# A chunked mLSTM cell and an MLP: float64 weights converted on ScalarE and VectorE alone, beside the first up-blocks

## Chip, cores and metric

The kernel runs on one core of a Trainium2 chip. The metric is device time in microseconds, the median of several executions; a profiled execution gives the span from its first to its last instruction. The engines are PE (TensorE: matmuls, with PEld for its weight loads), DVE (VectorE), ACT (ScalarE), POOL (GpSimd) and SP (SyncE, which here only issues DMAs). Each works through its own queue in order and waits on semaphores.

## The reference, cut

```python
# q, k, v, o_gate: (4, 8, 768, 40) float32; i_gate, f_gate: (4, 8, 768)
for t in range(S):
    m_new = np.maximum(f_gate[:, :, t] + m, i_gate[:, :, t])
    f_stab = np.exp(f_gate[:, :, t] + m - m_new)
    i_stab = np.exp(i_gate[:, :, t] - m_new)
    m = m_new
    C = f_stab[:, :, None, None] * C + i_stab[:, :, None, None] * np.einsum('bhd,bhe->bhde', vt, kt)
    n = f_stab[:, :, None] * n + i_stab[:, :, None] * kt
    h_tilde = np.einsum('bhde,bhe->bhd', C, qt)
    nq = np.einsum('bhd,bhd->bh', n, qt)[:, :, None]
    denom = np.maximum(np.abs(nq), 1.0)
    o = 1.0 / (1.0 + np.exp(-o_gate[:, :, t]))
    y[:, :, t] = o * h_tilde / denom
# x = y as (4 * 768, 320); w_in (320, 2048) and w_out (2048, 320) are float64
h = x @ w_in
g = h * (1.0 / (1.0 + np.exp(-1.702 * h)))
return (g @ w_out).astype(np.float32)
```

## The kernel before

The sequence is cut into six windows of 128 steps. A window holds 128 steps of all four batches, so 512 tokens. Inside a window the recurrence is done as attention with a decay matrix, plus a product with the state carried over from the window before. The order of all work is written out by hand; each engine's queue gets its instructions in program order.

For each window and batch there are these steps. `transposes` turns k and q (tiles p_t in PSUM, copied to kT by ACT and to qT by DVE). `columns` turns the gate columns, and its last line takes an exponential of the output gate's tile eo, for the whole window at once. `weights` builds the decay matrix wt (p_w on PE, 32 exponentials a window on ACT). `scores` multiplies q and k (p_s) and DVE multiplies the result into wt. `values` forms p_o and then y, the gated output (den, eo and y on DVE). `seam` transposes y (p_x) into xT. `carry` updates the state (vw on POOL, p_c on PE, state on DVE). `gates` does the running sums and maxima of the next window on DVE.

The MLP of a window has eight blocks `up(w, j)`: 12 issued matmuls in the profile's count into two p_h tiles, two gelus on ACT into a tile g. Then come 16 steps `down(w, b, n)`, four blocks of f (128 rows of w_out) each, into p_out, a copy o_sb and a DMA. The attention of window w+1 is run beside `down` of window w. `carry` and `transposes` stand between the up-blocks. In window 0 nothing runs ahead of the attention, so that its whole chain (transposes to seam) stands before the first up-block.

The weights come as float64, as pairs of 32-bit words, cut into pieces. A piece is a DMA into a tile bits, and a conversion to float32 into w_in_sb, w_in_x or w_out_sb. Up-block j of window 0 needs pieces 0 to 2 (j = 0, 1), also 3 and 4 (j = 2, 3), also 5 to 7 (j = 4, 5) and also 8 and 9 (j = 6, 7). Pieces from 10 on are w_out. In the kernel before, ten w_out pieces make 20 in all.

A conversion takes two steps on ACT (`convert_a`, one piece ahead), five on DVE and two on POOL (`convert_b`), and then fetches the piece that is ten further. The tiles bits and g share one ring of ten buffers (tag "g"), and the PSUM tiles of the attention (p_t, p_w, p_s, p_o, p_x, p_c, p_cols) share four buffers (tag "a"), taken in turn: a matmul into one waits until the tile four places earlier has been read. By the addresses of the built program, g of up-block j of window 0 takes the buffer of piece 10 + j before the change.

Of the kernel before, what the change touches and what calls it, by code (L numbers as in the profile page):

```python
# [16 lines left out]
# The cell's recurrence in chunks of L steps. With F the running sum of f_gate from the chunk's start,  # L17
# a = i_gate - F and M = max(m at the chunk's start, running max of a), the cell's m is F + M, and
#   h[t] = sum over s <= t in the chunk of exp(a[s] - M[t]) (k[s].q[t]) v[s] + exp(m0 - M[t]) C q[t],
# n likewise as a further column of v that holds ones. All exponents are at most 0. Products are float32.  # L20
#
# A window is one chunk of all batches: B * L tokens. Its attention runs beside the MLP of the window before.
L = 128
NEG = -1.0e30

# The MLP's weights come as float64, which no engine takes: the kernel gets their bits and makes float32 of them,
# rounded to nearest. As float32 numbers the high words compare as the weights do; what is below float32's normal
# range becomes 0, and what is above its largest value.
HI_MIN = 1.125 * 2.0 ** -15  # 0x38100000, the high word of 2**-126
HI_MAX = 15 * 2.0 ** 13 - 2.0 ** -7  # 0x47EFFFFF, the last before that of 2**128  # L30
# [3 lines left out]
def kernel(  # L34
# [31 lines left out]
    op = ctx.enter_context(tc.tile_pool(name="op", bufs=3))  # L66
# [17 lines left out]
    def load(w):  # L84
        eo[w] = ld.tile([L, BH, D], FP, tag="eo", name="eo")
        for dst, src in ((k_st[w % 2], k), (q_st, q), (v_st[w % 2], v), (eo[w], o_gate)):
            nc.sync.dma_start(out=dst[:, :, 0:D],
                              in_=src[:, :, w * L:(w + 1) * L, :].rearrange("b h s d -> s (b h) d"))

    # Pieces of the weights: words, low and high in turn, and where their float32 goes.  # L90
# [12 lines left out]
    def piece_out(f, n, m0, m1):  # L103
        return w_out_sb[:, f:f + n, m0:m1], [(slice(0, 128), out_bits[:, f:f + n, 2 * m0:2 * m1])]
# [4 lines left out]
    for n in range(8):  # L109
        pieces += [piece_out(2 * n, 2, 0, 256)] + ([piece_out(2 * n, 8, 256, DM)] if n % 4 == 0 else [])  # L110
# [11 lines left out]
    load(0)  # L122
# [13 lines left out]
    # neg_mask[s, t] = NEG where s > t.  # L136
# [4 lines left out]
    # pick[32 j + r, bh] = -1 where r == bh: minus the sum of three rows of m3 to all partitions.  # L141
# [4 lines left out]
    # half[bh, p] = 1 where p is in the half of bh's parity, pair[bh, j] = 1 where bh // 2 == j.  # L146
# [10 lines left out]
    # The states' transposes, two heads a block: [keys, values and the ones] in the diagonal blocks.  # L157
# [8 lines left out]
    def words(n):  # L166
        lo, hi = bits[n][:, :, :, 0], bits[n][:, :, :, 1]
        return lo, hi, lo.bitcast(FP), hi.bitcast(FP), pieces[n][0]

    def convert_a(n):  # L170
        lo, hi, lo_f, hi_f, dst = words(n)
        A.activation(out=dst, in_=hi_f, func=AF.Square)
        A.activation(out=lo_f, in_=lo, func=AF.Copy, scale=2.0 ** -52)

    def convert_b(n):
        # The high word with 8 bits of exponent, then the low word by the power of two that its exponent stands for.
        lo, hi, lo_f, hi_f, dst = words(n)
        dst_u = dst.bitcast(U32)
        V.scalar_tensor_tensor(out=hi_f, in0=dst, scalar=HI_MIN * HI_MIN, in1=hi_f, op0=OP.is_ge, op1=OP.mult)
        V.tensor_scalar(out=hi_f, in0=hi_f, scalar1=HI_MAX, scalar2=-HI_MAX, op0=OP.min, op1=OP.max)  # L180
        V.tensor_scalar(out=dst_u, in0=hi, scalar1=3, scalar2=0x3FFFFFFF, op0=OP.logical_shift_left,
                        op1=OP.bitwise_and)
        V.scalar_tensor_tensor(out=hi, in0=hi, scalar=0xC0000000, in1=dst_u, op0=OP.bitwise_and, op1=OP.bitwise_or)
        V.tensor_scalar(out=dst_u, in0=hi, scalar1=0xFF800000, scalar2=None, op0=OP.bitwise_and)
        G.tensor_tensor(out=dst, in0=lo_f, in1=dst, op=OP.mult)
        G.tensor_tensor(out=dst, in0=hi_f, in1=dst, op=OP.add)

    def convert(n):
        if n + 1 < len(pieces):
            convert_a(n + 1)  # L190
        convert_b(n)
        if n + RING < len(pieces):
            fetch(n + RING)

# [1 line left out]
    def gates(w):  # L196
# [33 lines left out]
    def columns(w):  # L230
# [11 lines left out]
        A.activation(out=eo[w], in_=eo[w], func=AF.Exp, scale=-1.0)  # L242

# [32 lines left out]
    def values(w, b):  # L276
# [7 lines left out]
        if w:  # L284
# [7 lines left out]
            V.tensor_tensor(out=u, in0=po, in1=u, op=OP.add)  # L292
        den = work.tile([L, H, 1], FP, tag="den", name="den")
        V.tensor_scalar(out=den, in0=u[:, :, D:D1], scalar1=-1.0, scalar2=1.0, op0=OP.mult, op1=OP.max)
        V.tensor_tensor(out=den, in0=u[:, :, D:D1], in1=den, op=OP.max)
        z = eo[w][:, hs, :]
        V.scalar_tensor_tensor(out=z, in0=z, scalar=1.0, in1=den.to_broadcast([L, H, D]), op0=OP.add, op1=OP.mult)  # L297
        V.reciprocal(out=z, in_=z)  # L298
        y = ys[w, b] = work.tile([L, DM + 64], FP, tag="y", name="y")
        V.tensor_tensor(out=y[:, 0:DM].rearrange("p (h d) -> p h d", d=D), in0=u[:, :, 0:D], in1=z, op=OP.mult)  # L300
        G.tensor_copy(out=y[:, DM:DM + 64], in_=y[:, DM - 64:DM])  # L301

    def seam(w, b):
        if b == 0:
            xT[w] = work.tile([128, 3, B, L], FP, tag="xT", name="xT")
        px = ps_a.tile([128, 3, L], FP, tag="a", name="p_x")
        for c in range(3):
            T.transpose(px[:, c, :], ys[w, b][:, c * 128:(c + 1) * 128], ident)  # L308
        A.copy(out=xT[w][:, :, b, :], in_=px)  # L309
# [52 lines left out]
    # What needs the exponential, of the next window, stands beside the second product, that which needs the  # L362
    # gelu beside the first: the activation tables change twice a window.
# [13 lines left out]

    gates(0)
    convert_a(0)
    for b in range(B):  # L380
        transposes(0, b)
    load(1)
    n_in = RING
    for n, step in enumerate(attention(0)):
        run(step)
        if n:
            convert(n - 1)
    for n in range(n, n_in + 1):
        convert(n)
    for w in range(NW):  # L390
        more = w + 1 < NW
        for j in range(NF // 2):
            up(w, j)
            if w == 0:
                convert(n_in + 1 + j)
                if j == NF // 2 - 1:
                    convert(len(pieces) - 1)
            if more:
                if j == 0:
                    gates(w + 1)  # L400
# [4 lines left out]
        if w + 2 < NW:  # L405
            load(w + 2)
        side = attention(w + 1) if more else []
        for n in range(B * NF // 4):
            down(w, n // (NF // 4), n % (NF // 4))
            if n % 2 == 0 and side:  # L410
                run(side.pop(0))
# [32 lines left out]
```

## Time and profile before

| What | Value |
|---|---|
| median of 3 runs | 687.8 us (687.78 to 689.64) |
| span of the profiled execution | 686.1 us |
| PE busy | 617.4 us, 90% of the span |
| DVE / ACT / POOL busy | 266.6 / 173.5 / 91.3 us |
| DMA moved | 30.35 MB on SP's queue |

The span is the profiled execution's own time from the first to the last instruction; the median of the runs is 1.7 us above it. Busy lines give tenths of 40 equal slices of 17.2 us each; PEclk gives the granted clock of TensorE in the same way. A row of a timeline begins with its start in us from the span's start and its length; the bracket gives the idle time of that engine before it and what ended it. A row of stages gives for each engine the busy time and the number of instructions, then the granted clock, the DMA share and the rate.

### The profile page before, as it was taken

How to read it: one execution, taken by the hardware profiler on the slowest of the kernel's cores; microseconds unless marked ns; L12 is line 12 of the kernel's file. 1: busy time of each engine (PE TensorE's matmuls, PEld its weight loads, DVE VectorE, ACT ScalarE, POOL GpSimd, SP SyncE). 2: the span in 40 equal slices, each digit the busy share in tenths (PEclk: the TensorE clock that was granted, in tenths of full speed). 3: DMA queues.
4: the chain of work that ended last, by engine and by line, in shares of the span. 5: the costliest groups of instructions: out<-in, count | busy, mean ns of one | idle time of the engine just before them, and what ended most of it. 6: DMA issues, size and time to landing. Idle time of an engine off the chain costs nothing.

```text
span 686.1 us, 7417 instructions
## 1 busy us (share of the span) xinstructions
PE 617.4 (90%) x2950; PEld 390.1 (57%) x2950; DVE 266.6 (39%) x501; ACT 173.5 (25%) x404; POOL 91.3 (13%) x116
## 2 busy tenths in 40 slices
PE   2566317899999999999999999999999999999998
PEld 2454113357774457874457864467864467853475
DVE  3588994451663111663102562103561114630000
ACT  0642222253302242311233211242111242112200
POOL 2233653341002000011000011000011000000000
PEclk9755659999999999999999999999999999999999
DMA  9995220328000336000355000373000000000000
GB/s 138 312 164 165 92 62 0 39 27 99 11 10 11 39 41 85 11 11 10 39 58 67 11 21 0 40 76 49 11 20 0 1 3 14 5 20 0 0 20 19
DMA packets 108770, 30.81 MB, mean 45 GB/s; under 512 B 99456, under 2 KB 105600, under 8 KB 108736
## 3 DMA queue, kind: packets, MB, share of 16 engines
q1 hardware_dynamic: 108736, 30.35, 27.2%
q8 instruction: 23, 0.38, 0.2%
q14 instruction: 11, 0.09, 0.0%
HBM read 26.41 MB, written 3.93 MB: 44 GB/s over the span
## 4 chain that ended last, share of the span: by engine, by line
PE 78%; DVE 3%; issue 0%; POOL 0%; DVEq 0%
PE p_out L354 27%; PE p_h L341 22%; PE p_h L344 7%; PE p_o L282 5%; PE p_s L272 3%; PE p_t L250 3%; PE p_i L287 3%; PE p_c L319 3%; DVE eo L298 2%; PE p_w L258 1%; PE p_w L261 1%; PE p_x L308 1%; DVE u L291 0%; DVE u L292 0%; DVE y L300 0%; DVE eo L297 0%
## 5 line engine op out<-in xcount | busy, mean ns | idle before, releaser
L354 PE MATMUL p_out<-w_out_sb,g 128*128 128x320 f32 x768 | 216.6, 436 | 0.0
L341 PE MATMUL p_h<-xT,w_in_sb 128*128 128x512 f32 x384 | 179.9, 612 | 0.6 <-ACT xT L309 0.6
L354 PEld LDWEIGHTS p_out<-w_out_sb,g 128*128 128x128 f32 x768 | 142.6, 190 | 55.1 <-issue 0.8
L341 PEld LDWEIGHTS p_h<-xT,w_in_sb 128*128 128x128 f32 x384 | 71.8, 196 | 79.3 <-issue 71.2
L347 ACT ACTIVATE g<-p_h 128x512 f32<-128x512 f32 x96 | 52.1, 595 | 203.1 <-PE p_h L344 201.3
L265 ACT ACTIVATE wt<-p_w,cols 128x128 f32<-128x128 f32 x192 | 52.4, 386 | 94.2 <-PE p_w L261 94.2
L301 POOL COPY y<-y 128x64 f32<-128x64 f32 x24 | 6.0, 250 | 394.5 <-DVE y L300 394.5
L358 DVE COPY o_sb<-p_out 128x320 f32<-128x320 f32 x24 | 11.7, 486 | 120.0 <-PE p_out L354 120.0
L252 DVE COPY qT<-p_t 128x512 f32<-128x512 f32 x24 | 16.6, 691 | 98.9 <-PE p_t L250 98.9
L344 PE MATMUL p_h<-xT,w_in_x 64*128 64x512 f32 x192 | 54.2, 641 | 0.0
L319 PE MATMUL p_c<-vw,k_st 128*128 128x82 f32 x160 | 23.8, 295 | 31.7 <-POOL vw L315 31.7
L298 DVE RECIPROCAL eo<-eo 128x320 f32<-128x320 f32 x24 | 51.7, 2153 | 0.8
L282 PEld LDWEIGHTS p_o<-v_st,wt 128*128 128x128 f32 x384 | 50.7, 209 | 1.6 <-issue 0.2
L282 PE MATMUL p_o<-v_st,wt 128*128 128x41 f32 x384 | 51.3, 295 | 0.0
L319 PEld LDWEIGHTS p_c<-vw,k_st 128*128 128x128 f32 x160 | 20.6, 201 | 47.2 <-POOL vw L315 35.1
L309 ACT COPY xT<-p_x 128x384 f32<-128x384 f32 x24 | 11.5, 477 | 123.5 <-PE p_x L308 123.5
L291 DVE TENSOR_TENSOR u<-p_i,cols 128x328 f32<-128x328 f32 x20 | 10.0, 499 | 78.5 <-PE p_i L287 78.5
L274 DVE TENSOR_TENSOR wt<-p_s,wt 128x512 f32<-128x512 f32 x48 | 30.9, 682 | 14.3 <-PE p_s L272 14.1
L344 PEld LDWEIGHTS p_h<-xT,w_in_x 64*128 64x128 f32 x192 | 14.5, 184 | 36.4 <-issue 36.4
L330 DVE TENSOR_TENSOR state<-p_c,state 64x164 f32<-64x164 f32 x32 | 10.4, 326 | 63.5 <-PE p_c L319 63.3
L272 PE MATMUL p_s<-qT,kT 40*128 40x128 f32 x384 | 30.0, 299 | 0.0
L272 PEld LDWEIGHTS p_s<-qT,kT 40*128 40x128 f32 x384 | 25.2, 201 | 3.8 <-issue 2.4
(93 smaller groups left out, 480.7 us busy)
## 6 DMA issues: line engine op xcount, KB each, us to landing
bits<-in_moe_w_out_dram SPq DMA_DIRECT2D x10, 512.0 KB, 4.0
bits<-in_moe_w_in_dram SPq DMA_DIRECT2D x8, 512.0 KB, 7.7
k_st<-in_k_dram SPq DMA_DIRECT2D x6, 640.0 KB, 6.4
q_st<-in_q_dram SPq DMA_DIRECT2D x6, 640.0 KB, 6.7
v_st<-in_v_dram SPq DMA_DIRECT2D x6, 640.0 KB, 10.1
eo<-in_o_gate_dram SPq DMA_DIRECT2D x6, 640.0 KB, 10.2
out_dram<-o_sb SPq DMA_DIRECT2D x24, 160.0 KB, 1.8
bits<-in_moe_w_in_dram SPq DMA_DIRECT2D x4, 256.0 KB, 8.0
```

The source lines that it names most:

```text
L250: T.transpose(pt[:, p, :], src[:, h:h + 2, :].rearrange("p a b -> p (a b)"), ident)
L265: A.activation(out=x[:, i, p, :], in_=pw[:, p, :], func=AF.Exp, bias=cols[w][:, h:h + 1])
L272: T.matmul(pw[i][:, p, :], kT[w, b][r, p, :], qT[w, b][r, p, :], start=True, stop=True)
L274: V.tensor_tensor(out=wt[w, b][:, i], in0=pw[i], in1=wt[w, b][:, i], op=OP.mult)
L282: T.matmul(po[:, h, :], wt[w, b][:, i, p, :], v_st[w % 2][:, b * H + h, :], start=True, stop=True)
L287: T.matmul(pi[:, 2 * p:2 * p + 2, :].rearrange("p a b -> p (a b)"), qT[w, b][:, p, :], state[w % 2][:, b * NP + p].rearrange("p a b -> p ( ...
L298: V.reciprocal(out=z, in_=z)
L319: T.matmul(pc[:, p].rearrange("p a b -> p (a b)"), k_st[w % 2][:, h:h + 2, :].rearrange("p a b -> p (a b)"), vw[:, 2 * p:2 * p + 2, :].rea ...
L341: T.matmul(ph[i], w_in_sb[:, c, f * 128:(f + 1) * 128], x[:, c, :], start=(c == 0), stop=False)
L344: T.matmul(ph[i], w_in_x[r, j, :], x[r, 2, :], start=False, stop=True)
L347: A.activation(out=g[:, i, :], in_=ph[i], func=AF.Gelu_apprx_sigmoid)
L354: T.matmul(po, gs[w, f // 2][:, f % 2, b * L:(b + 1) * L], w_out_sb[:, f, :], start=(f == 0), stop=(f == NF - 1))
```

## The change

The conversion loses its POOL steps and becomes two steps on ACT and four on DVE, with an exact integer addition at the end. The w_out pieces become eight of 128 x 2 x 320, 18 pieces in all. Conversions are no longer interleaved with the first window's attention: pieces 0 to 2 stand beside its last seams, 3 to 15 beside up-blocks 0 to 6 (a table `beside_up` says which pieces are converted and which are fetched behind each block), and 16 and 17 beside the first two down steps. The first window's attention runs all weights and scores first and then all values and seams. `gates(1)` moves from block 0 to block 5. The load of the second window is cut in two parts: k and q after the first transposes, v and the output gate behind the fetches of block 1. The first window's 16 down steps go by halves of f: all batches with f 0 to 7, then all with f 8 to 15. The sigmoid is made of tanh (0.5 (1 + tanh(x/2))), and the reciprocal is taken of the eight denominators of a batch in place of 320 products. xT has one buffer for two, o_sb two for three.

```diff
-    def convert_a(n):
-        A.activation(out=dst, in_=hi_f, func=AF.Square)
-        A.activation(out=lo_f, in_=lo, func=AF.Copy, scale=2.0 ** -52)
-    def convert_b(n):
-        V.scalar_tensor_tensor(out=hi_f, in0=dst, scalar=HI_MIN * HI_MIN, in1=hi_f, op0=OP.is_ge, op1=OP.mult)
-        V.tensor_scalar(out=hi_f, in0=hi_f, scalar1=HI_MAX, scalar2=-HI_MAX, op0=OP.min, op1=OP.max)
-        V.tensor_scalar(out=dst_u, in0=hi, scalar1=3, scalar2=0x3FFFFFFF, op0=OP.logical_shift_left,
-        V.scalar_tensor_tensor(out=hi, in0=hi, scalar=0xC0000000, in1=dst_u, op0=OP.bitwise_and, op1=OP.bitwise_or)
-        V.tensor_scalar(out=dst_u, in0=hi, scalar1=0xFF800000, scalar2=None, op0=OP.bitwise_and)
-        G.tensor_tensor(out=dst, in0=lo_f, in1=dst, op=OP.mult)
-        G.tensor_tensor(out=dst, in0=hi_f, in1=dst, op=OP.add)
+    def convert(n):
+        A.activation(out=dst, in_=hi.bitcast(FP), func=AF.Abs)
+        A.activation(out=lo, in_=lo, func=AF.Copy, scale=2.0 ** -29)
+        V.tensor_scalar(out=dst, in0=dst, scalar1=HI_MIN, scalar2=HI_MAX, op0=OP.max, op1=OP.min)
+        V.tensor_scalar(out=dst_u, in0=dst_u, scalar1=3, scalar2=0x3FFFFFFF, op0=OP.logical_shift_left,
+        V.scalar_tensor_tensor(out=dst_u, in0=hi, scalar=0xC0000000, in1=dst_u, op0=OP.bitwise_and,
+        V.tensor_tensor(out=dst_u, in0=dst_u, in1=lo, op=OP.add)
...
-        A.activation(out=eo[w], in_=eo[w], func=AF.Exp, scale=-1.0)
+        A.activation(out=eo[w], in_=eo[w], func=AF.Tanh, scale=0.5)
...
+        V.reciprocal(out=den, in_=den)
         z = eo[w][:, hs, :]
-        V.scalar_tensor_tensor(out=z, in0=z, scalar=1.0, in1=den.to_broadcast([L, H, D]), op0=OP.add, op1=OP.mult)
-        V.reciprocal(out=z, in_=z)
+        V.scalar_tensor_tensor(out=z, in0=z, scalar=1.0, in1=u[:, :, 0:D], op0=OP.add, op1=OP.mult)
-        V.tensor_tensor(out=y[:, 0:DM].rearrange("p (h d) -> p h d", d=D), in0=u[:, :, 0:D], in1=z, op=OP.mult)
+        V.scalar_tensor_tensor(out=y[:, 0:DM].rearrange("p (h d) -> p h d", d=D), in0=z, scalar=0.5,
+                               in1=den.to_broadcast([L, H, D]), op0=OP.mult, op1=OP.mult)
...
-    load(1)
-    n_in = RING
-    for n, step in enumerate(attention(0)):
-        run(step)
-        if n:
-            convert(n - 1)
-    for n in range(n, n_in + 1):
-        convert(n)
+    load(1, 0)
+    columns(0)
+    for b in range(B + 1):
+        if b < B:
+            weights(0, b)
+        if b:
+            scores(0, b - 1)
+    for b in range(B + 1):
+        if b < B:
+            values(0, b)
+        if b:
+            seam(0, b - 1)
+            if b <= 3:
+                convert(b - 1)
+    beside_up = [((3, 4), (10, 11)), ((5, 6), (12, 13)), ((7, 8), (14,)), ((9, 10), (15,)), ((11, 12), (16,)),
+                 ((13, 14), (17,)), ((15,), ()), ((), ())]
...
+            blocks = [(b, n) for n0 in range(0, NF // 4, 2) for b in range(B) for n in (n0, n0 + 1)]
```

ACT at the program's start, before the change (kT, cols, eo, wt belong to the attention, the others to conversions):

```order
L172 ACT_TABLE_LOAD
L172 ACTIVATE w_in_sb<-bits 128x512
L173 ACTIVATE bits<-bits 128x512
L252 COPY kT<-p_t 128x512 x4
L239 ACTIVATE cols<-p_cols 128x64
L242 ACTIVATE eo<-eo 128x1280
L265 ACTIVATE wt<-p_w,cols 128x128 x8
```

and after it:

```order
L238 ACT_TABLE_LOAD
L238 COPY kT<-p_t 128x512 x4
L225 ACTIVATE cols<-p_cols 128x64
L228 ACTIVATE eo<-eo 128x1280
L251 ACTIVATE wt<-p_w,cols 128x128 x32
L297 COPY xT<-p_x 128x3x128
L172 ACTIVATE w_in_sb<-bits 128x512
```

The first conversion step has moved from ahead of the kT copies to behind all 32 exponentials and the first xT.

POOL around the first up-blocks, before (L185 and L186 are conversion steps, vw feeds p_c of `carry`):

```order
L185 TENSOR_TENSOR w_out_sb<-bits,w_out_sb 128x8x64
L186 TENSOR_TENSOR w_out_sb<-bits,w_out_sb 128x8x64
L315 TENSOR_TENSOR vw<-v_st_86,cols 128x328
L185 TENSOR_TENSOR w_out_sb<-bits,w_out_sb 128x2x256
L186 TENSOR_TENSOR w_out_sb<-bits,w_out_sb 128x2x256
```

and ACT behind the gelu of up-block 1 after the change, with buffer numbers (g_567 is up-block 2, bits_109 to bits_116 are pieces 5 to 8, g_601 is up-block 3):

```order
L335 ACTIVATE g_528<-p_h_521 128x512
L172 ACTIVATE w_in_sb_88<-bits_109 128x512
L173 ACTIVATE bits_109<-bits_109 128x512
L172 ACTIVATE w_in_sb_88<-bits_111 128x512
L173 ACTIVATE bits_111<-bits_111 128x512
L335 ACTIVATE g_567<-p_h_559 128x512
L335 ACTIVATE g_567<-p_h_560 128x512
L172 ACTIVATE w_in_x_89<-bits_113 128x512
L173 ACTIVATE bits_113<-bits_113 128x512
L172 ACTIVATE w_in_sb_88<-bits_116 128x512
L173 ACTIVATE bits_116<-bits_116 128x512
L335 ACTIVATE g_601<-p_h_593 128x512
```

vw has no conversion ahead of it on POOL any more, and two pieces' ACT steps stand between two gelus. By the addresses of the built program g of up-blocks 0 to 7 now takes the buffers of pieces 0, 3, 6, 8, 10, 12, 14 and 15.

DVE between the last block that has a state copy and the end of the up-blocks, after the change (the rows of w_out_sb are one piece, 15; ISA is the integer addition, over 1280 halves of 640 words):

```order
L208 TENSOR_TENSOR left_710<-left_705,part_707 32x128
L204 CAST part_712<-left_710 32x128
L205 COPY m3_701<-part_712 32x128
L213 TENSOR_TENSOR both_716<-m_end_163,m_run_692 32x1
L214 TENSOR_SCALAR dec_715<-pair_145,both_716 32x16
L238 COPY qT_731<-p_t_726 128x512
L174 TENSOR_SCALAR w_out_sb_90<-w_out_sb_90 128x640
L175 TENSOR_SCALAR w_out_sb_90<-w_out_sb_90 128x640
L177 SCALAR_TENSOR_TENSOR w_out_sb_90<-bits_616,w_out_sb_90 128x640
L179 ISA w_out_sb_90<-bits_616,w_out_sb_90 128x1280
L238 COPY qT_762<-p_t_757 128x512
L238 COPY qT_787<-p_t_782 128x512
```

and before it, the rows at the same place:

```order
L252 COPY qT_800<-p_t_795 128x512
L179 SCALAR_TENSOR_TENSOR bits_557<-w_out_sb_90,bits_557 128x512
L180 TENSOR_SCALAR bits_557<-bits_557 128x512
L181 TENSOR_SCALAR w_out_sb_90<-bits_557 128x2x256
L183 SCALAR_TENSOR_TENSOR bits_557<-bits_557,w_out_sb_90 128x512
L184 TENSOR_SCALAR w_out_sb_90<-bits_557 128x2x256
L252 COPY qT_834<-p_t_829 128x512
```

The qT copy of the second batch now stands behind the next window's gates, which stood ahead of the first state copy.

More of the change, by code (lines that the diff above doesn't have):

```diff
@@ L82, with load @@
     w_out_sb = const.tile([128, NF, DM], FP, name="w_out_sb")
-    def load(w):
-        eo[w] = ld.tile([L, BH, D], FP, tag="eo", name="eo")
-        for dst, src in ((k_st[w % 2], k), (q_st, q), (v_st[w % 2], v), (eo[w], o_gate)):
+    def load(w, part):
+        if part:
+            eo[w] = ld.tile([L, BH, D], FP, tag="eo", name="eo")
+        for dst, src in (((v_st[w % 2], v), (eo[w], o_gate)) if part else ((k_st[w % 2], k), (q_st, q))):
             nc.sync.dma_start(out=dst[:, :, 0:D],
@@ L121 @@
     nc.sync.dma_start(out=i_sb, in_=i_gate.rearrange("b h s -> (b h) s"))
-    load(0)
+    load(0, 0)
+    load(0, 1)
     for n in range(RING):
@@ L394 @@
             if w == 0:
-                convert(n_in + 1 + j)
-                if j == NF // 2 - 1:
-                    convert(len(pieces) - 1)
+                for n in beside_up[j][0]:
+                    convert(n)
+                for n in beside_up[j][1]:
+                    fetch(n)
+                if j == 1:
+                    load(1, 1)
             if more:
-                if j == 0:
+                if j == (5 if w == 0 else 0):
                     gates(w + 1)
```

39 lines of the change are left out of this document (17 added, 22 removed).

## The prediction

> **What bounds the kernel now.** I read the slices of the page first, then stages of the span, then who waits in the thin stage.
>
> ```profile
> PE   2566317899999999999999999999999999999998
> PEclk9755659999999999999999999999999999999999
> 67.00:74.00 7.00, 7.00 (x12) 2.57 (x12) 6.79 (x9) 5.63 (x10) 4.25 (x3) 0.68 0.22 76
> 74.00:99.50 25.50, 0.00 (x0) 0.00 (x0) 24.73 (x29) 3.47 (x5) 16.97 (x13) 0.59 0.29 83
> 99.50:150.50 51.00, 44.75 (x149) 21.76 (x150) 25.88 (x58) 15.41 (x29) 19.11 (x17) 0.91 0.12 13
> 500.00:600.00 100.00, 99.41 (x498) 63.01 (x498) 32.87 (x66) 25.06 (x60) 6.57 (x12) 1.00 0.02 7
> ```
>
> ```profile
> 94.43 1.08 ACT L347 ACTIVATE g<-p_h 128x512 f32<-128x512 f32 x2 [1.83 <-POOL w_out_sb L186]
> 98.62 0.85 POOL L315 TENSOR_TENSOR vw<-v_st,cols 128x328 f32<-128x328 f32 x1
> 99.53 2.00 PE L319 MATMUL p_c<-vw,k_st 128*128 128x82 f32 x8 [25.53 <-POOL vw L315]
> 150.45 2.32 PE L354 MATMUL p_out<-w_out_sb,g 128*128 128x320 f32 x8
> ```
>
> PE is full only from the ninth slice on; late in the run it is busy 99.4 of 100 us, so there no other engine's work can shorten anything. The loss is ahead of 150.45, where the first down product starts. Block 0 of up (67 to 74) is followed by 25.5 us without one matmul: DVE converts (24.73 busy), the gelu waits for a piece of w_out in its buffer, and vw, which p_c needs, stands behind the conversions on POOL. I forecast the new time of that down product and carry the rest over.
>
> **Durations that a conversion is made of.**
>
> ```profile
> 26.22 0.43 DVE L180 TENSOR_SCALAR bits<-bits 128x512 f32<-128x512 f32 x1
> 27.15 0.69 DVE L183 SCALAR_TENSOR_TENSOR bits<-bits,w_in_sb 128x512 uint32<-128x512 uint32 x1
> 68.06 1.63 POOL L185 TENSOR_TENSOR w_in_sb<-bits,w_in_sb 128x512 f32<-128x512 f32 x1 [2.15 <-DVE w_in_sb L184]
> 68.56 1.41 DVE L180 TENSOR_SCALAR bits<-bits 128x512 f32<-128x512 f32 x1
> ```
>
> A tensor-scalar step takes 0.43, but 1.41 where a POOL multiplication runs beside it. POOL's 40 conversion steps go, so I take 0.43. A new piece is on DVE two of these, one step with two operands (0.69), and the integer add, each with 0.03 between: the add is in no row. It reads two tensors of 512 words, as the 0.69 row does, but is issued over 1024 halves: 0.69 if two halves pass together, about 1.22 if singly (0.53 more at the 0.53 that 512 elements cost). I take 0.85, nearer to the row with the same bytes, and keep both ends. That makes 2.5 us a piece of w_in. A piece of w_out has 640 words; from 0.49 for 320 and 0.69 for 512 (rows below) 128 more cost 0.13, half that for tensor-scalar, 0.16 for the add: 2.95. Abs and Copy replace Square and Copy on ACT at the same 0.66 (row at 21.92), 0.56 apart.
>
> The Trainium skill (Vector Engine (DVE) Microarchitecture Reference, section 5.1) says that two-source instructions on 2-byte elements with unit steps pass two elements a cycle. By that rule the add would take 0.69, and the forecast would be about 2 us lower; no row here has such an instruction.
>
> **Start of block 0: 67.0 to 47.5.**
>
> ```profile
> 10.09 4.63 SPq L87 DMA_DIRECT2D eo<-in_o_gate_dram  x1
> eo<-in_o_gate_dram SPq DMA_DIRECT2D x1, 640.0 KB, 10.5
> 13.23 1.11 PE L250 MATMUL p_t<-ident,q_st 128*128 128x128 f32 x4 [3.57 <-DMA q_st<-in_q_dram]
> 21.92 0.66 ACT L172 ACTIVATE w_in_sb<-bits 128x512 f32<-128x512 f32 x1 [19.90 <-DMA bits<-in_moe_w_in_dram]
> 23.02 2.03 ACT L252 COPY kT<-p_t 128x512 f32<-128x512 f32 x4
> 25.74 1.26 ACT L242 ACTIVATE eo<-eo 128x1280 f32<-128x1280 f32 x1
> 26.90 2.17 ACT L265 ACTIVATE wt<-p_w,cols 128x128 f32<-128x128 f32 x8
> ```
>
> ACT's first Square waits for the first weights and holds the four kT copies to 23.0. It goes; q landed at 13.2, and eight transposes about 0.85 apart with their copies end near 19.6. What is late next is o_gate: it lands at 10.09 + 10.5 = 20.6, and the tanh (priced as the exponential, 1.26) stands ahead of the weights' exponentials on ACT. They start at 21.9, 2.0 per batch, nothing between them now: 29.9.
>
> ```profile
> 29.56 2.04 PE L282 MATMUL p_o<-v_st,wt 128*128 128x41 f32 x16
> 38.72 3.71 PE L282 MATMUL p_o<-v_st,wt 128*128 128x41 f32 x16
> 31.53 1.16 PE L272 MATMUL p_s<-qT,kT 40*128 40x128 f32 x16
> 42.35 2.08 PE L272 MATMUL p_s<-qT,kT 40*128 40x128 f32 x16
> 53.08 0.17 DVE L294 TENSOR_SCALAR den<-p_o 128x8 f32<-128x8 f32 x1 [2.82 <-PE p_o L282]
> 53.48 0.49 DVE L297 SCALAR_TENSOR_TENSOR eo<-eo,den 128x320 f32<-128x320 f32 x1
> 54.01 2.15 DVE L298 RECIPROCAL eo<-eo 128x320 f32<-128x320 f32 x1
> 56.26 0.49 DVE L300 TENSOR_TENSOR y<-p_o,eo 128x320 f32<-128x320 f32 x1
> 65.36 1.07 PE L308 MATMUL p_x<-ident,y 128*128 128x128 f32 x3 [4.14 <-DVE y L300]
> 66.47 0.48 ACT L309 COPY xT<-p_x 128x384 f32<-128x384 f32 x1 [7.08 <-PE p_x L308]
> ```
>
> The last scores need the last exponentials (their buffers): 1.16 warm, 2.08 cold, I take 1.6, to 31.5. Then p_o of batch 0, 2.04 to 3.71, I take 2.9, to 34.4. From there DVE sets the pace. A y costs two den steps (0.2 each with the gap), a reciprocal of 128x8 (between the 0.17 of a den step and 8/320 of 2.15 on top of it: 0.2), and two 0.49 steps: 1.65 where it was 3.7. DVE then runs y0, y1, piece 0, y2, piece 1, y3: 4 x 1.65 + 2 x 2.5 = 11.6, to 46.0. POOL's copy, p_x and xT (0.25 + 0.7 + 0.48) give 47.5. Piece 2 ends at 48.5; only the block's last two matmuls need it. All warm gives 46.2; all cold (each p_o 3.7, each p_x 1.07, DVE waiting for them, y3 at 50.7) 52.5.
>
> **Block 0 to the first down product: 76.4 to 47.9.** Block 0 itself I leave at 7.0, partly cold: end 54.5, from which t counts.
>
> ```profile
> 144.01 0.66 PE L250 MATMUL p_t<-ident,k_st 128*128 128x128 f32 x4
> 149.52 0.66 PE L250 MATMUL p_t<-ident,k_st 128*128 128x128 f32 x4
> 134.10 0.69 DVE L252 COPY qT<-p_t 128x512 f32<-128x512 f32 x1 [3.23 <-PE p_t L250]
> 2.94 0.41 DVE L202 TENSOR_TENSOR_SCAN f_run<-one,f_sb 32x128 f32<-32x128 f32 x1 [0.62 <-DMA f_sb<-in_f_gate_dram]
> 7.81 0.19 DVE L219 COPY m<-part 32x128 bf16<-32x128 bf16 x1
> ```
>
> PE needs 5.5 us per block with what stands behind it, 39.5 in all. DVE and the buffers need more. Gelu j may write only when the piece whose buffer it takes is converted (3, 6, 8, 10, 12, 14, 15 for j = 1 to 7), and the next two pieces' Abs stand behind that gelu on ACT: 1.8 from gelu's start to Abs done. A state or qT copy is 0.7; gates take 4.2 (the 5.1 seen from 2.94 to 8.0, less a wait and one slow step, plus the decay).
> - gelu 0, Abs: t = 1.8. Pieces 3, 4, state: 7.5. Pieces 5, 6: 12.5, state 13.2.
> - gelu 2 after piece 6, Abs 14.4; pieces 7, 8: 19.4. gelu 3, Abs 21.3; pieces 9, 10: 26.8, state.
> - gelu 4, Abs 28.8; pieces 11, 12: 34.7, qT. gelu 5, Abs 36.7; pieces 13, 14: 42.6; gates 46.8; qT 47.4.
> - The last p_t takes the buffer which that qT copy frees: 47.4, and 0.5 later the first down product.
>
> So DVE's queue, not PE, ends this stage, with PE idle near 8 us. The w_in pieces stay ahead of their blocks (piece 7 at 16.9, block 4 at 17.3). With the add at 1.22 the same steps end at 52.8, at 0.69 at 46. Fetches: pieces 12 and 13 wait on SP for pieces 4 and 5; then the loads of v and o_gate pass (4.63 each); piece 14 leaves near t = 20 and even 10.5 later is 6 ahead of its Abs. Hidden, as is w_out in eight fetches for ten.
>
> ```profile
> 101.32 5.81 PE L341 MATMUL p_h<-xT,w_in_sb 128*128 128x512 f32 x8
> 118.47 3.64 PE L341 MATMUL p_h<-xT,w_in_sb 128*128 128x512 f32 x8
> 153.11 4.57 PE L354 MATMUL p_out<-w_out_sb,g 128*128 128x320 f32 x16
> PE p_x L308 <- DVE y L300: 2.9, 5, 0.6
> ```
>
> **Behind it.** After a pause PE starts cold (5.81 for 3.64); a pause near 7 us ahead of down costs 2.2 again. Pieces 16 and 17 end at t = 62; in the new order the ninth group of four down steps needs them, eight groups of 2.3 after 47.9, with attention between: covered. The one xT buffer is written in down, after the last block has read it; the two o_sb are free again when the transfer of two groups earlier is out: nothing for either. The tanh brings no further table load in the program's order. In later windows the shorter y only removes the five waits of the last p_x: 2.9.
>
> **Sum.** Down product at 47.5 + 7.0 + 47.9 + 2.2 = 104.6 for 150.45: 45.9 less, and 2.9 less later. 686.1 - 48.8 = 637.3 of span. The median of the runs (687.8) stands 1.7 over the profiled span: 639.
>
> The Trainium skill (TensorE: Matmul & The Clock Gate, Part 1) has the clock drop after one idle window of about 3.4 us and return after one busy one. By that rule the waits near 2 us would stay warm and only the pause ahead of down is paid, as in the sum; attention paced by ACT could stay cold, the 52.5 of the start, and the time would be 644.
>
> **Rivals.**
> - The buffers bind less than I think and PE alone sets the blocks: 47.9 becomes 39.5 and the cold restart goes, 628. For it: POOL is empty. Against: DVE's own work there, 12 pieces (32), six state or qT copies (4) and gates (4), is 41 before any wait, so the add would have to be 0.69 as well.
> - The 1.41 comes from something other than POOL (the rows at 26.22 and 68.56 speak against it): 2 x 0.98 on 14 pieces, 27 more: 666.
> - Fetches late: if v and o_gate crawl, piece 14 arrives after t = 36.7; ten us late is 649, twenty 659.
> - Slower than before: the add runs like RECIPROCAL, 2153/320 = 6.7 ns an element, 6.9 us a piece. Fourteen pieces on the chain (9 of w_in, 5 wider) then cost over 90 more: about 730. It decides from an add of about 4 us. Against it: simple steps of two tensors all run near 1 ns.
> - Nothing gained: the conversions set the old pace. Only with two of these together.
>
> **Numbers.** Chances: forecast 0.78, PE alone 0.09, slow tensor-scalar 0.05, late fetches 0.04, slow add 0.03, nothing 0.01. Low end: warm start, add 0.69, no cold restart give 633.5; half of the PE rival brings 629. High end: cold start (+5), add 1.22 (+4.9), slow steps in gates (+2.3) give 651; a little of a late fetch, 654. That holds eight in ten. The runs before spread 0.3%, so 0.3% is about what can be told from nothing: faster 0.95, same 0.02, slower 0.03.
>
> **What would show it.** First wt exponential on ACT near 21.9, behind tanh; block 0 near 47.5; the add at 0.7 to 1.2 and tensor-scalars at 0.43; gelu 2 to 6 released by DVE, not by PE; first down product near 102 to 107; p_x without waits in later windows. The forecast falls if the add is above 1.5, if Abs waits for DMA, or if PE runs cold far beyond block 0.

## The result and the profile after

The changed kernel takes 639.48 us (median of 4 runs, 637.7 to 640.22) where the kernel before took 687.8 beside it (687.78 to 689.64): 0.9291 of the time, with a 95% interval of 0.9272 to 0.9309. The profiled execution has a span of 638.4 us for 686.1.

The page of the changed kernel, its line of busy times and the slices of PE and of the granted clock (16 us each):

```profile
PE 614.4 (96%) x2950; PEld 391.5 (61%) x2950; DVE 192.2 (30%) x473; ACT 173.7 (27%) x400; POOL 37.1 (6%) x76
...
PE   2898997999999999999999999999999999999997
...
PEclk9756997999999999999999999999999999999999
```

PE is busy 70% or more of every slice from the second on. The clock is another matter: slices two to four show 0.7, 0.5 and 0.6 though PE is busy there. The same by stages (span part, length, PE's busy time and instructions, granted clock, DMA share, GB/s):

```profile
20.00:25.00 5.00, 2.22 (x26) 1.00 1.07 311
25.00:30.00 5.00, 5.00 (x34) 0.50 1.02 389
...
35.00:40.00 5.00, 5.00 (x26) 0.50 1.38 175
55.00:60.00 5.00, 5.00 (x9) 0.58 0.38 131
60.00:65.00 5.00, 5.00 (x20) 1.00 0.00 0
```

PE pauses from about 20.8 to 23.0 and once more, for 0.55, up to 24.0. At 25.0 the clock falls, and from there PE runs without a gap until 50 and at half clock until 59; ahead of block 0 it waits 1.22 for the last y and 0.57 for xT. The timeline of that stretch and of the first up-block (start, length, engine, line):

```profile
21.82 4.23 ACT L251 ACTIVATE wt<-p_w,cols 128x128 f32<-128x128 f32 x16
30.87 3.79 PE L258 MATMUL p_s<-qT,kT 40*128 40x128 f32 x32
34.59 7.05 PE L268 MATMUL p_o<-v_st,wt 128*128 128x41 f32 x32
43.43 0.43 DVE L174 TENSOR_SCALAR w_in_sb<-w_in_sb 128x512 f32<-128x512 f32 x1 [0.28 <-ACT w_in_sb L172]
45.19 0.69 DVE L179 CUSTOM_DVE_ANT_0 w_in_sb<-bits,w_in_sb 128x1024 uint16<-128x1024 uint16 x1
52.94 6.77 PE L329 MATMUL p_h<-xT,w_in_sb 128*128 128x512 f32 x8 [0.57 <-ACT xT L297]
59.64 1.13 PE L332 MATMUL p_h<-xT,w_in_x 64*128 64x512 f32 x4
```

The p_o of two batches takes 7.05, at half clock throughout; a conversion's first step is back at 0.43 and the integer addition (CUSTOM_DVE_ANT_0) takes 0.69. Block 0 starts at 52.94 where it started at 67 before. The end of the up-blocks:

```profile
101.36 0.41 DVE L188 TENSOR_TENSOR_SCAN f_run<-one,f_sb 32x128 f32<-32x128 f32 x1
101.53 1.09 ACT L335 ACTIVATE g<-p_h 128x512 f32<-128x512 f32 x2 [3.19 <-DVE w_out_sb L179]
103.83 0.58 ACT L238 COPY kT<-p_t 128x512 f32<-128x512 f32 x1
104.46 1.11 PE L236 MATMUL p_t<-ident,q_st 128*128 128x128 f32 x4 [3.98 <-ACT kT L238]
105.37 4.47 PE L342 MATMUL p_out<-w_out_sb,g 128*128 128x320 f32 x8
105.57 0.67 DVE L238 COPY qT<-p_t 128x512 f32<-128x512 f32 x1
```

The gelu of block 6 waits for a w_out piece on DVE, the kT copy stands behind that gelu and the next Abs, and the last p_t waits 3.98 for it. Then down begins at 105.37 (150.45 before), at half clock. From there to the end, before and after in one row each (PE, PEld, DVE, ACT, POOL busy, clock, DMA share, GB/s):

```profile
150.45:686.10 535.65, 529.52 (x2579) 335.76 (x2577) 165.10 (x324) 126.08 (x304) 30.96 (x55) 1.00 0.19 26
```

```profile
105.37:638.40 533.03, 529.76 (x2578) 337.12 (x2577) 130.48 (x335) 128.41 (x307) 27.24 (x52) 1.00 0.19 27
```

So 45.1 us of the 47.7 came ahead of the first down product, and 2.6 behind it.

### The profile page after: what moved, and what is told of

Read it like the earlier page. It is cut to its first block, busy times and chain, and to the rows that moved or that the text cites. A ratio compares the mean times of both kernels' runs of the same rounds, so it can differ in the third digit from the quotient of the medians.

```text
span 638.4 us, 7322 instructions
## 1 busy us (share of the span) xinstructions
PE 614.4 (96%) x2950; PEld 391.5 (61%) x2950; DVE 192.2 (30%) x473; ACT 173.7 (27%) x400; POOL 37.1 (6%) x76
## 4 chain that ended last, share of the span: by engine, by line
PE 89%; DVE 4%; DMA 3%; ACT 2%; SPq 1%; issue 0%; DVEq 0%; ACTq 0%
PE p_out L342 33%; PE p_h L329 23%; PE p_h L332 7%; PE p_o L268 7%; PE p_s L258 5%; PE p_i L273 3%; PE p_c L307 3%; PE p_t L236 3%; PE p_w L244 2%; PE p_w L247 2%; DMA eo<-in_o_gate_dram 2%; PE p_x L296 1%; SPq L88 1%; DMA v_st<-in_v_dram 1%; ACT g L335 1%; DVE w_out_sb L177 1%
## 5 line engine op out<-in xcount | busy, mean ns | idle before, releaser
L329 PE MATMUL p_h<-xT,w_in_sb 128*128 128x512 f32 x384 | 177.4, 605 | 0.6 <-ACT xT L297 0.6
L236 PEld LDWEIGHTS p_t<-ident,k_st 128*128 128x128 f32 x96 | 11.7, 155 | 23.7 <-issue 23.7
L236 PE MATMUL p_t<-ident,k_st 128*128 128x128 f32 x96 | 17.2, 307 | 8.6 <-DMA k_st<-in_k_dram 8.6
```

The costliest lines, as they stand in the source:

```text
L236: T.transpose(pt[:, p, :], src[:, h:h + 2, :].rearrange("p a b -> p (a b)"), ident)
L329: T.matmul(ph[i], w_in_sb[:, c, f * 128:(f + 1) * 128], x[:, c, :], start=(c == 0), stop=False)
```

## The experiments

All of them are edits of the changed kernel. Spans are those of the profiled executions, to be compared with 638.4.

### What the parts are worth

**The old conversion in the new places.** The conversion's body is that of before (Square, Copy, five DVE steps, two POOL steps), the table `beside_up` and all else as changed.

```diff
-        A.activation(out=dst, in_=hi.bitcast(FP), func=AF.Abs)
+        A.activation(out=dst, in_=hi_f, func=AF.Square)
...
-        V.tensor_tensor(out=dst_u, in0=dst_u, in1=lo, op=OP.add)
+        G.tensor_tensor(out=dst, in0=lo_f, in1=dst, op=OP.mult)
+        G.tensor_tensor(out=dst, in0=hi_f, in1=dst, op=OP.add)
```

> Edit: the conversion as before the change (five DVE steps and two on POOL a piece), in the changed kernel's order and places. Theory A (the steps themselves set the pace: 4.65 us a piece on DVE before the change, two tensor-scalars of 1.40 among them beside POOL's products, for 2.45 now): twelve pieces 3 to 14 take 7 x 2.2 and 5 x 2.7 longer, 29 in all, less the 4 that DVE waited for ACT; first down product near 130, block 0 up to 3 later; span 660 to 668. Rival B (the order gave the gain: conversions spread beside the blocks hide behind PE whichever way they are made): span 638 to 648.

717.2 us, 1.0419 of before (1.0399 to 1.044): the new order with the old conversion is slower than the kernel before. Neither theory had that. Its timeline behind block 0:

```profile
66.30 0.66 ACT L173 ACTIVATE w_in_sb<-bits 128x512 f32<-128x512 f32 x1
69.93 1.62 POOL L181 TENSOR_TENSOR w_in_sb<-bits,w_in_sb 128x512 f32<-128x512 f32 x1 [8.91 <-issue]
70.44 1.40 DVE L176 TENSOR_SCALAR bits<-bits 128x512 f32<-128x512 f32 x1
75.95 1.29 POOL L182 TENSOR_TENSOR w_in_sb<-bits,w_in_sb 128x512 f32<-128x512 f32 x1
77.20 0.73 POOL L306 TENSOR_TENSOR vw<-v_st,cols 128x328 f32<-128x328 f32 x1
77.98 2.00 PE L310 MATMUL p_c<-vw,k_st 128*128 128x82 f32 x8 [14.01 <-POOL vw L306]
79.78 4.58 PE L332 MATMUL p_h<-xT,w_in_sb 128*128 128x512 f32 x8
100.03 4.69 PE L332 MATMUL p_h<-xT,w_in_sb 128*128 128x512 f32 x8
```

Block 1 stands behind p_c on PE, p_c waits for vw, and vw stands on POOL behind the conversion of two pieces, which begins behind the gelu of block 0. A block thus waits for a whole round through ACT, DVE and POOL: 20.3 us from one to the next (79.78, 100.03). In the changed kernel vw has nothing ahead of it on POOL. The row at 70.44 also shows the tensor-scalar at 1.40 again, beside a POOL product that runs from 69.93: the 1.40 does come from POOL.

**The old output gate.** Exponential on ACT, reciprocal of 128x320, as before.

```diff
-        A.activation(out=eo[w], in_=eo[w], func=AF.Tanh, scale=0.5)
+        A.activation(out=eo[w], in_=eo[w], func=AF.Exp, scale=-1.0)
...
-        V.reciprocal(out=den, in_=den)
...
+        V.reciprocal(out=z, in_=z)
```

> Edit: the output gate as before the change (exponential on ACT, reciprocal of 128x320 on DVE), all else as changed. Theory A (the gate's chain y, p_x, xT ends the steady windows and the first chunk): in the five later windows the wait of the last p_x comes back, 0.6 to 1.0 each, 3 to 5 in all; in the first chunk a y takes 3.7 for 1.5 on DVE, so DVE's 11 become 19.7 and block 0 begins 6 to 8 later; span 647 to 652. Rival B (PE's slow products set the first chunk and hide the longer y): only the later windows lose, span 641 to 643.

651.2 us (0.9458 of before, 0.9438 to 0.9479), span 649.2. Theory A. Block 0 begins 6.8 later, and from the first down product on the kernel takes 4.8 longer than the 533.03 above:

```profile
59.74 6.01 PE L328 MATMUL p_h<-xT,w_in_sb 128*128 128x512 f32 x8 [0.57 <-ACT xT L296]
```

```profile
111.38:649.20 537.82, 531.63 (x2578) 336.82 (x2577) 171.63 (x335) 128.25 (x307) 27.21 (x52) 1.00 0.19 27
```

```profile
PE p_x L295 <- DVE y L287: 2.9, 5, 0.6
```

The last row (who waits for whom: us in total, times, longest) is the wait that before had and the changed kernel has not. It is 2.9 of the 4.8; the other 1.9 is PE's busy time (531.63 for 529.76).

**The old order of the first window's attention.** One step of weights, scores, values and seams of successive batches, as before; pieces 0 to 2 in its last steps.

```diff
-    columns(0)
-    for b in range(B + 1):
...
+    for n, step in enumerate(attention(0)):
+        run(step)
+        if 4 <= n <= 6:
+            convert(n - 4)
```

> Edit: the first chunk's attention in the order of before (weights of batch s, scores of s-1, outputs of s-2, transposes of s-3 in one step), with pieces 0 to 2 converted in its last steps; all else as changed. Theory A (the order's lockstep costs waits, as before the change where PE stood still for some 10 of the 38 us between 29 and 67): block 0 begins at 56 to 60, span 642 to 646. Theory B (PE's cold products set the first chunk, and they are the same ones): block 0 within 1.5 of 52.9, span 637 to 640.

638.82 us (0.9278 of before, 0.9261 to 0.9295), span 637.9; block 0 at 53.38 for 52.94. Theory B: this part of the change is worth nothing that can be measured here. PE goes from 25 to 50 at half clock in both orders; what the order is worth at full clock was not tried.

**The natural order of the first down groups.**

```diff
-            blocks = [(b, n) for n0 in range(0, NF // 4, 2) for b in range(B) for n in (n0, n0 + 1)]
```

> Edit: the first window's down groups in their natural order (all four groups of a batch after one another), so that the fourth group needs pieces 16 and 17, which in the changed kernel are finished at 114.2 and 119.3. Theory A (the new order hides them): the fourth group would start near 115 and waits for piece 17, 4 to 5 us, span 642 to 644. Theory B (attention between the groups, at half clock, hides them anyway): no change, span 638 to 639.

644.25 us (0.9357 of before, 0.9341 to 0.9374), span 642.9, so the new order is worth 4.5. Theory A; the fourth group waits for piece 17:

```profile
119.53 5.19 PE L342 MATMUL p_out<-w_out_sb,g 128*128 128x320 f32 x12 [2.76 <-DVE w_out_sb L179]
```

The wait is 2.76 of the 4.5. The rest is PE at half clock behind it (0.50 from 120 to 123): these twelve products take 5.19, where 16 take 4.53 in the changed kernel.

### What sets the blocks

**Abs and Copy ahead of the block.** They leave their place behind gelu j.

```diff
+            if w == 0:
+                for n in beside_up[j][0]:
+                    convert_act(n)
             up(w, j)
             if w == 0:
                 for n in beside_up[j][0]:
-                    convert(n)
+                    convert(n, act=False)
```

> Edit: the Abs and Copy steps of the pieces that stand behind gelu j on ACT are put ahead of block j instead. Theory A (a loop sets the stage: a gelu waits on its buffer for a piece, the Abs of the next two pieces wait behind that gelu, and DVE waits about 1.1 us a block for them): the loop opens, DVE's waits for ACT go, pieces 3 and 4 are done during block 0, PE sets the blocks at some 5.5 us each. First down product 99 to 101 instead of 105.4, and its cold restart (2.3) goes too: span 631 to 634 for 638.4. Rival B (DVE's own work, about 40 us, sets the stage whatever the order): the first down product comes at most 2 us earlier, the pause ahead of it and the cold restart stay, span 636 to 638. Rival C (the early Abs find their weights not yet landed and hold the gelus back): slower, Abs waiting for DMA on ACT.

632.8 us (0.9189 of before, 0.9173 to 0.9206), span 631.1. Theory A, to the number. In the changed kernel DVE waited for these steps of ACT, and the gelus waited for DVE:

```profile
DVE w_in_sb L174 <- ACT w_in_sb L172: 9.1, 2, 8.0
DVE w_out_sb L174 <- ACT w_out_sb L172: 2.4, 2, 1.2
```

The 8.0 is one wait, for the Abs of piece 3 behind gelu 0; the others are near 1.1 a block. So the moved steps do two things: pieces 3 and 4 are converted while block 0 runs, and the wait in each later block goes. No run separates the two.

With the steps moved, such waits are gone, the gelus wait for PE alone, and down starts 5 us earlier and at full clock (2.32 for 4.47):

```profile
77.50 1.09 ACT L339 ACTIVATE g<-p_h 128x512 f32<-128x512 f32 x2 [1.99 <-PE p_h L336]
...
100.47 2.32 PE L346 MATMUL p_out<-w_out_sb,g 128*128 128x320 f32 x8
```

Block 0 ends at 60.8 in both; from there to down it is 39.7 us here and 44.6 in the changed kernel.

**No integer addition.** The low word is not added; its products and everything else stay.

```diff
-        V.tensor_tensor(out=dst_u, in0=dst_u, in1=lo, op=OP.add)
```

> Leaves out the integer addition of the low word in every piece (the weights lose their last bits), nothing else. If the chain of pieces sets the blocks, the twelve pieces 3 to 14 are each 0.69 (0.83 for w_out) and a gap of 0.1 shorter: about 10 us less chain, of which PE's own 39.5 us for the blocks lets 5 through, and the cold restart of 2.3 goes as well: first down product at 99 to 101, span 631 to 633. If DVE does not set the stage: no change, 638. Block 0's start: earlier by up to 1.6 if DVE sets it (two pieces stand ahead of the last y), unchanged at 52.9 if PE's slow products do.

631.89 us (0.9177 of before, 0.9159 to 0.9196), span 629.7; first down product at 99.06, at full clock, block 0 from 52.71 to 59.3.

```profile
99.06 2.32 PE L341 MATMUL p_out<-w_out_sb,g 128*128 128x320 f32 x8
```

So the chain of pieces did set the blocks: taking some 10 us out of it brings them to PE's own 39.8, and no further. Block 0's start does not move: there it is not DVE that sets the pace. Block 0 itself is 1.2 shorter, because in this execution the clock rose at 56.4 and not at 59.2.

**The gates one block later.**

```diff
-                if j == (5 if w == 0 else 0):
+                if j == (6 if w == 0 else 0):
```

> Edit: the gates of the second window stand behind block 6 instead of block 5 on DVE. The prediction's step (the last p_t takes the buffer which the qT copy behind the gates frees, so the 4.2 of gates lie on the path): the first down product comes up to 4 us earlier, at 101 to 102, span 634 or less. The reading of the trace after (the last p_t takes the buffer which the kT copy on ACT frees, behind gelu 6, which waits for piece 14; pieces 13 and 14 stand ahead of the gates): no change, first down product 105 to 106, span 638 to 639; if anything slower, since the columns of the second window need the gates.

642.68 us (0.9331 of before, 0.9307 to 0.9355), span 641.0: slower by 2.6, which neither reading gave. The last p_t and with it the first down product come earlier (102.21 for 105.37), near what the prediction's step gave, but the second down group stands behind the gate columns on PE, and these now wait for the gates:

```profile
101.72 0.65 PE L236 MATMUL p_t<-ident,q_st 128*128 128x128 f32 x4 [1.62 <-DVE qT L238]
102.21 2.32 PE L342 MATMUL p_out<-w_out_sb,g 128*128 128x320 f32 x8
107.84 0.27 PE L218 MATMUL p_cols<-ident,st 96*128 96x96 f32 x1 [3.32 <-DVE st L198]
110.06 0.60 PE L222 MATMUL p_cols<-dec,half 32*128 32x16 f32 x2 [1.95 <-DVE dec L214]
```

The edit also changes which buffer the last p_t takes. By the addresses of the two built programs it is here the buffer of q of batch 1, four places earlier, which the qT copy frees at 101.7; in the changed kernel it is that of k of batch 2, three places earlier, which the kT copy frees at 104.4. So the rule "taken in turn, four places earlier" of the section on the kernel does not hold for that tile, and the gates at block 5 are not free: they do not stand in the chain that ends at the first down product, but with them out of the way of that qT copy it begins 3.2 earlier. At block 6 they cost more than that: the waits of 3.32 and 1.95, and a group at half clock behind them.

### What sets the start

**The tanh behind the exponentials.**

```diff
-        A.activation(out=eo[w], in_=eo[w], func=AF.Tanh, scale=0.5)
+        if w:
+            A.activation(out=eo[w], in_=eo[w], func=AF.Tanh, scale=0.5)
...
+    A.activation(out=eo[0], in_=eo[0], func=AF.Tanh, scale=0.5)
     for b in range(B + 1):
         if b < B:
             values(0, b)
```

> Edit: the first window's tanh of the o_gate stands behind all 64 exponentials of the weights on ACT instead of ahead of them. Theory A (the exponentials on ACT, held by the tanh and the landing of o_gate, set the start): exponentials begin near 20.0 instead of 21.8, block 0 begins 1.8 earlier at 51.1, span 636.6. Theory B (from the first scores at 30.9 on, PE's own cold products set the start): the scores may begin up to 1.8 earlier too, so the same gain, unless DVE's y, which now waits for the tanh near 31, or kT and qT copies hold them: then block 0 stays at 52.9. The two agree if PE starts with the exponentials; they part if the scores stay at 30.9.

632.15 us (0.9192 of before, 0.915 to 0.9233), span 629.1. Block 0 begins at 46.34, 6.6 earlier and not 1.8. PE's pause is gone (0.31 for 2.23 ahead of the first scores), and the clock stays full until 32.3, 2.3 after p_o began:

```profile
25.00:30.00 5.00, 4.76 (x59) 1.00 1.03 383
30.00:35.00 5.00, 5.00 (x34) 0.73 1.08 249
35.00:40.00 5.00, 5.00 (x27) 0.50 1.39 206
```

The same scores that took 3.79 for two batches take 1.16 a batch here. That raised the question whether the 1.8 on ACT or the clock gave the gain.

**Ten idle matmuls in the pause.** Their result is read by nobody.

```diff
+    def warm(k):
+        pd = ps_m.tile([128, W], FP, tag="m", name="p_d")
+        for i in range(k):
+            T.matmul(pd, ident_b, neg_mask.unsqueeze(1).to_broadcast([L, NP, L]), start=(i == 0), stop=(i == k - 1))
...
             weights(0, b)
+        if b == 1:
+            warm(10)
```

> Edit: ten 128x512 bfloat16 matmuls into a spare PSUM tile are put on PE behind the weights' products of batch 1, where PE in the changed kernel stands still from 20.7 to 23.0. Their result is not read. Theory A (that pause makes the clock fall at 25.0): the clock stays at 1.00 through the scores, p_s and p_w run at full speed as in the run with the late tanh (clock full until 32.3, block 0 at 46.3), and block 0 begins 1.7 later than there because the exponentials begin 1.7 later: 48.0 for 52.9; span 633 to 634. Theory B (the clock falls because the scores with 40 rows and the weights' products load PE lightly, pause or not): the fall stays near 25, block 0 at 52.9 or a little later, span 638 to 639.

633.07 us (0.9205 of before, 0.9173 to 0.9238), span 631.8, block 0 at 47.03. The ten products, the clock while the scores run, and block 0:

```profile
20.63 2.32 PE L370 MATMUL p_d<-neg_mask,ident_b 128*128 128x512 bf16 x10
30.00:35.00 5.00, 4.80 (x53) 1.00 1.08 264
47.03 6.29 PE L329 MATMUL p_h<-xT,w_in_sb 128*128 128x512 f32 x8 [0.57 <-ACT xT L297]
```

Theory A: useless products that fill the pause, and nothing else changed, give 5.9 us at the start, and each of the four runs (632.51 to 636.95) is below each of the changed kernel's (637.7 to 640.22). So of the late tanh's 6.6 most is the clock.

**And six more ahead of each step of p_o and p_x.**

```diff
+        warm(6)
         if b < B:
             values(0, b)
         if b:
             seam(0, b - 1)
```

> Edit: the ten matmuls of the run before, and six more of them ahead of each of the five steps of p_o and p_x in the first chunk. Theory A (41 columns a product keep the clock down though PE is never idle, wide products keep it up): the clock stays at 1.00 to block 0; p_o takes 2.0 a batch for 3.5, six matmuls 1.3 a step, so PE needs 3.9 a step and DVE (four y of 1.5, two pieces of 2.45) 11 in all: last y near 44.8, block 0 near 46.5 and 4.8 long for 7.8, its end near 51 for 60.7; span 628 to 630. Theory B (the clock falls in this stretch whatever PE does): six matmuls cost 2.6 a step at half clock, block 0 later than 52.9, span above 640.

634.66 us (0.9207 of before, 0.9179 to 0.9236), span 633.5, where 628 to 630 was expected. In this execution the ten products ended 0.91 ahead of the first scores, the clock fell at 26.7 all the same, and the gain of the run before was lost: filling the pause does not keep the clock every time. But the question it was made for is answered:

```profile
34.09 2.74 PE L370 MATMUL p_d<-neg_mask,ident_b 128*128 128x512 bf16 x6
36.63 2.02 PE L268 MATMUL p_o<-v_st,wt 128*128 128x41 f32 x16
39.78 1.87 PE L268 MATMUL p_o<-v_st,wt 128*128 128x41 f32 x16
...
52.24 3.70 PE L329 MATMUL p_h<-xT,w_in_sb 128*128 128x512 f32 x8 [0.57 <-ACT xT L297]
```

With 512-column products between them the clock rises at 36.9, in the middle of the attention, and p_o runs at 1.87 a batch to the end for 3.48; block 0 takes 3.70 for 6.77 in its first eight.

### A faster version

**Late tanh and early Abs together**, and the same with six idle matmuls a step:

> Two edits together: the first window's tanh behind the exponentials of the weights, and Abs and Copy of the pieces ahead of their block on ACT. If the two gains are of different places (start of block 0: 9.3 of span; blocks and cold restart: 7.3, of which the late-tanh run may already hold part of the restart), block 0 begins near 46.3, the first down product 39 to 40 after block 0's end at 92 to 93, span 621 to 624. If the earlier start moves the blocks into the landing of the weights (Abs waiting for DMA), the gains overlap: span 625 to 629.

> As the run before, with six 128x512 bfloat16 matmuls, whose result is not read, ahead of each of the five steps of p_o and p_x. From the run with kept clock: p_o 1.87 for 3.48 and block 0 4.8 for 6.8 to 7.8 long. If the clock is still full at 30 (as with the late tanh), the first p_o ends near 33.4, DVE's 11 us set the rest, block 0 begins at 45 to 46 and ends near 50.5 for 52.6: span 2 us under the run before, 619 to 622. If the matmuls only take PE's time: the same or up to 3 longer.

The first takes 625.58 us (median of 6 runs, 624.66 to 629.71; 0.9103 of before, 0.9077 to 0.9129), span 623.1, block 0 at 46.30 and down at 92.45, at full clock:

```profile
92.45 2.32 PE L347 MATMUL p_out<-w_out_sb,g 128*128 128x320 f32 x8
```

The two gains lie in different places and add up, 13.9 us under the changed kernel. The second takes 626.75 (626.38 to 627.71; 0.9106, 0.9092 to 0.9121), span 625.3, and is not faster: the clock had fallen at 24.6, ahead of the first of its idle matmuls, with block 0 at 50.19. Up to there the two programs are the same.

## Why the prediction held, and where it was wrong

The time came out at 639.5 for 639.0, but that it came so close is luck: terms that were too small and terms that were too large cancelled. Step by step, in the prediction's own terms:

- **First exponential near 21.9, behind the tanh.** 21.82. Right: with the tanh behind them the exponentials begin at 20.17. But that is 1.65 earlier, and block 0 came 6.6 earlier, so most of it is the clock.
- **Start of block 0, 47.5: wrong by 5.4.** It was 52.94. The step that failed is the choice of a middle between warm and cold durations (at full and at half clock) for p_s and p_o ("I take 1.6", "I take 2.9"). There was no middle in the profiled execution: the clock fell at 25.0 and all that followed ran cold, as in the bound of 52.5 that I had worked out and given as the high end. The sentence on the clock rule of the Trainium skill (TensorE: Matmul & The Clock Gate, Part 1) had put 52.5 beside an attention that stays cold, and so it came; the total of 644 that went with it did not, because of the terms below. What that rule was taken to say of the waits, that near 2 us they would stay warm, did not come: the clock fell 2.0 us after the end of a wait of 2.23. With the middle fell "from there DVE sets the pace": without the addition, DVE has less to do and block 0 starts within 0.3 us of the same place (52.71).
- **Block 0, 7.0.** 7.8, for the same reason.
- **Block 0 to the first down product, 47.9.** 44.6. The mechanism, that a gelu waits for a piece and the next Abs for that gelu, is shown by the moved Abs (39.7, PE's own pace, where the prediction had 39.5 for PE) and by the run without addition. Two terms were off. The addition was priced at 0.85 and takes 0.69, for which the prediction itself had 46. And the last step named the wrong releaser: the last p_t took the buffer which the kT copy on ACT freed at 104.4, not the one of the qT copy behind the gates, which began only at 105.6. That the gates' place holds the first down product back was still near the truth: one block later, it comes 3.2 earlier.
- **Cold restart of down, 2.2.** 4.47 for 2.32: right, though the pause ahead of it was 3.98 and not near 7.
- **Behind it, 2.9 less.** 4.8 less by the run with the old gate; the p_x waits were counted, PE's busy time was not. With the cold restart that gives the 2.6 between the rows above.
- **Sum.** 5.4 and 0.8 too little, 3.3 and 1.9 too much: 638.4 for 637.3.

Of the rivals, "PE alone sets the blocks" did not hold for this change, but one move of two ACT steps made it hold. The slow tensor-scalar from another cause than POOL is refuted by 0.43 in the changed kernel and 1.40 in the run with the old conversion. Late fetches and a slow addition did not come: no Abs waits for a DMA in the changed kernel, and the addition takes 0.69. What no rival had is that the order without the new conversion would be a loss: 717.2 for 687.7.

The rule of the Trainium skill (Vector Engine (DVE) Microarchitecture Reference, section 5.1), by which such an addition passes two halves a cycle, agrees with the measured 692 ns for 1024 halves, the same as the two-operand step over 512 words.

## What to carry to other kernels

An order that hides work beside matmuls is worth what the hidden work's queue allows: the same placement lost 4% with a conversion that shared POOL with one small product on PE's path, and gained 7% without it. Where an engine's first step for the next piece stands behind a gelu that itself waits for the last piece, put it ahead: two moved lines gave nearly as much as taking an instruction of 0.69 us out of every piece. And read PEclk beside PE: a busy PE can run at half clock for 30 us, and a pause of 2 us ahead of narrow products can be dearer than the pause (here filling it gave 5.9 us at the start).

## What the hardware showed that was not expected

PE was busy without a gap from 25 to 50 in the changed kernel, with scores of 40 rows and p_o of 41 columns, and stayed at 0.50. In the run with the late tanh the clock was full when p_o began at 30.04 and fell at 32.3, with PE busy from 29 on. With 512-column products between, the same p_o kept full clock. So a busy PE alone does not keep the clock up here. The Trainium skill (TensorE: Matmul & The Clock Gate, Part 1) lets the clock drop after an idle window of about 3.4 us and return after a busy one; here a window full of narrow products acted like an idle one. Whether columns, rows, or the share of weight loads decides was not tried.

The pause goes with an early fall, but not strictly. In one profiled execution each, the eight kernels with the pause (the changed one and seven edits of it) lose the clock between 23.4 and 25.7; of the five whose pause is filled or gone, three keep it until 32.3, 32.6 and 35.2, and two lose it at 24.6 and 26.7.

The moments at which the clock changes are spaced by whole multiples of one length, and it is that of the free-running window of 3413 ns which the Trainium skill (TensorE: Matmul & The Clock Gate, Part 1) states. One-us rows of PE (busy, clock, DMA share, GB/s) in the changed kernel:

```profile
25.00:26.00 1.00, 1.00 (x7) 0.51 0.98 310
59.00:60.00 1.00, 1.00 (x4) 0.92 0.00 0
```

and in the last of the runs above, with idle matmuls in the faster version:

```profile
24.00:25.00 1.00, 1.00 (x9) 0.81 1.20 237
34.00:35.00 1.00, 1.00 (x6) 0.57 1.05 371
```

Since the rows beside them show 1.00 on one side and 0.50 on the other, a mean of 0.51 over a microsecond puts the fall at 25.02, and 0.92 the rise at 59.16: 34.14 apart, ten times 3.41. The second pair gives 24.62 and 34.86: 10.24, three times 3.41. The late tanh gives 17.08 (32.32 to 49.40), five times. The place of these steps differs from execution to execution, so that the same program keeps its clock through the scores in one run and loses it in another; that fits the spread of the runs with the late tanh (630.7 to 636.8) and of the faster version (624.7 to 629.7), and with the mean granted clock of these runs (0.984 at the fastest and 0.970 at the slowest of the first, 0.986 and 0.976 of the second). Only the profiled executions show the moments themselves.
